# Attention and soft mixture of experts on one core: the turned scores are fetched in whole blocks, exponentials, z, v and weights come at other times

## The chip, the cores and the metric

The kernel runs on one core of a Trainium2 chip. The metric is the device time of one execution in microseconds: the median of three runs of the kernel before is 1449.97 us (1448.82 to 1451.36). The engines are TensorE (PE; PEld is its loading of weights), VectorE (DVE), ScalarE (ACT), GpSimd (POOL) and SyncE (SP). SP computes nothing: every DMA of this kernel is issued by SP, in program order, and SP waits in front of a DMA whose conditions aren't met. ACT and DVE, too, work through their instructions in the order in which the program issues them.

## The reference, cut to what matters

```python
scores = (1 / S) * np.matmul(z, z.transpose(0, 2, 1))     # 8 batches, S = 2496 tokens, z has 64 columns
attn = np.maximum(scores, 0.0) ** 2
x = (u * np.matmul(attn, v)).reshape(N, D)                # N = 19968 tokens, D = 256
logits = x @ phi                                          # 8 experts x 4 slots = 32 columns
d = np.exp(logits - logits.max(0)); d /= d.sum(0) + 1e-09
slot_input = d.T @ x                                      # 32 x 256, 4 slots to each expert
slot_out[e] = np.maximum(slot_input[e] @ w1[e], 0.0) @ w2[e]
c = np.exp(logits - logits.max(1)); c /= c.sum(1) + 1e-09
out = c @ slot_out
```

The score matrix of a batch is symmetric, because keys and queries are the same z. The kernel computes most blocks of it once and turns them over for the other side of the diagonal.

## The kernel before, in words

**Tiling.** A batch has five blocks of up to 512 tokens, and five chunks of queries by the same cut (the last block holds 448 tokens and is padded to 512). A chunk meets the five key blocks one after the other, and each key block in two halves of 256 keys. So a batch is 50 halves, numbered through by `h`; the last batch has 60, because its last chunk of queries is cut in two of 256. The list `MEETS` gives the order of key blocks for each chunk. In every batch but the first, a pair of a chunk and a key block is scored only for the side that comes first. When the other side comes, the half is a turned half: its scores are fetched.

**One half.** `scores` (line 253) gives two PSUM banks of scores, each float32 input split into a high and a low part (three products). In `prepare` (line 288), ACT applies relu with the scale, and squares; then the tile `r` is split again: a cast to `ph` by ACT or DVE, and a subtraction by DVE that gives `pl`. For a pair whose turned side comes later, DVE also turns `r` in squares of 32 x 32 into a tile `y` (line 323 and after), and after both halves of the pair `store` (line 332) writes `y` to a scratch tensor `turned` in HBM, with four DMAs of 256 KB. For a turned half, `fetch` (line 234) has brought `r` from `turned`, and `prepare` only casts and subtracts. `sums_halves` (line 352) or `sums_whole` (line 387, where the half to be prepared is turned) then multiply `ph` and `pl` with the high and low parts of v and add up in `acc`.

**The order of the work** is written out by hand in the loop over `halves` (line 695). While PE sums half `h`, half `h + 3` is prepared. `transfers(h)` (line 641) issues the DMAs: u for the chunk, the fetch for half `h + 5` if that is turned, loads of the next batch's z and v by the tables `z_at` and `v_at` (lines 633 and 634, in halves of the batch), and the stores that have become due. After it, one step of the list `work` runs, if the half is not one of the first two of its chunk. These steps are the mixture's work on a group of 1024 finished tokens (`groups`, line 447): logits on PE and their maxima on DVE; the exponentials on ACT (`exps`); turning x and the exponentials on DVE; four times four DMAs of 72 KB that shift the turned tokens over partitions (`xt<-y`); and the softmax over slots. What a step puts in the list `middle` runs inside the next `prepare`, between relu and square; what it puts in `behind` runs at its end.

**Buffers.** `r` has four, `ph` and `pl` five each, `y` two. z and v of a batch lie in a ring of 16 (`blk`). In the last 20 halves `weights` (line 600) loads the experts' weights, one or two for a half, into buffers that z, v and y leave; 20 of the 32 tiles come before the attention ends, the rest after it.

All compute and DMA instructions but a few pass one helper at line 59, so the rows of the profile name line 59 and are told apart by their tiles: `acc<-ph,v` are the sums, `sc<-z,z` the scores, `r<-turned` a fetch, `turned<-y` a store, `xt<-y` a shift, `zr<-in_zz` and `vr<-in_v` loads of z and v.

Of the kernel before, what the change touches and what calls it, by code (L numbers as in the profile page):

```python
# [34 lines left out]
NWX = 12  # L35
# [27 lines left out]
def attn_soft_moe_kernel(ctx, tc, uT, v, zz, phi, ww, outT):  # L63
# [26 lines left out]
    def take_blocks(b):  # L90


        order = BLOCKS[b == B - 1]
        for j in order[:-1]:
            zt[b, j] = blk.tile([P, 2, 512], F32R, tag="blk", name=f"z_{b}_{j}")
        for i in range(2 * NP):
            vt_[b, i] = blk.tile([P, 2, 2, D], F32R, tag="blk", name=f"v_{b}_{i}")
        j = order[-1]
        zt[b, j] = blk.tile([P, 2, 512], F32R, tag="blk", name=f"z_{b}_{j}")
# [77 lines left out]
    turns_sb = moe.enter_context(tc.tile_pool(name="turns_sb", bufs=2))  # L177
# [68 lines left out]

    def compact(t, x):
        n = x.ch[2]
        if x.padded:
            return t.rearrange("p h (g w) -> p h g w", g=2)[..., 0:PAD]  # L250
        return t[:, :, :n]
# [36 lines left out]
    def prepare(k):  # L288
# [5 lines left out]
        if x.turned:  # L294
            r = arriving.pop(k)
            run(middle)
        else:
            r = wa.tile([P, 2, QC], F32, tag="r", name=f"r_{k}", bufs=4)
            ps, m = scores(k)
            for h in parts:  # L300
                act.activation(r[:, h, :m], ps[:, h, :m], AF.Relu, scale=1.0 / S)
            run(middle)
            for h in parts:
                act.activation(r[:, h, :m], r[:, h, :m], AF.Square)
        hi, lo = (
            wa.tile([P, 2, QC], F32R, tag=t, name=f"{t}_{k}", bufs=5) for t in ("ph", "pl")
        )
        whole = compact(r, x)
        hc, lc = (
            t[:, :, :n].rearrange("p h (g w) -> p h g w", g=2) if x.padded else t[:, :, :n]  # L310
            for t in (hi, lo)
        )
# [35 lines left out]


    side = [0]  # L350

    def sums_halves(k, acc, phase, before):
# [3 lines left out]
        n = x.ch[2]  # L356
# [12 lines left out]
        for i in range(len(todo[0])):  # L369
            for h, rows in enumerate(HALF):  # L370
# [3 lines left out]
                    acc[:, c, :n], vp[rows, c * P : (c + 1) * P], pp[rows, :n],  # L374
# [12 lines left out]
    def sums_whole(k, acc):  # L387

        x = halves[k]
        n = x.ch[2]  # L390
        hi, lo = pend[k]
        for t, kt in enumerate(x.tiles):
            assert kt < KT - 1
            vt = vt_[x.b, kt // 2][:, kt % 2]
            for c in range(2):
                for i, (l, r) in enumerate(((0, hi), (1, hi), (0, lo))):
                    pe.matmul(
                        acc[:, c, :n], vt[:, l, c * P : (c + 1) * P], r[:, t, :n],
# [48 lines left out]
    def groups(q):  # L447
# [17 lines left out]
        def logits():  # L465
# [22 lines left out]
            middle.append(exps)  # L488
# [72 lines left out]
        c1 = lambda: middle.append(combine_exp)  # L561
        rest = lambda: None
        if q < NQG - 2:

            todo = [logits, *blocks, e, shifts[0], c0, shifts[1], c1, shifts[2], c2, shifts[3]]
            todo.append(lambda: (c3(), late.append(slot_sums)))
        else:
# [3 lines left out]
            todo = [*blocks[:2], rest, *blocks[2:], rest, logits, rest, e, lambda: (shifts[0](), add()), *shifts[1:]]  # L571
# [28 lines left out]
    def weights(i):  # L600
# [3 lines left out]
        if i == 0:  # L604
            for _ in range(NBLK):
                take_w(blk, "blk")
            for _ in range(2):
# [3 lines left out]
        order = [[k] for k in (0, 1, 2, 3, 4, 16, 17, 18, 19)] + [[], [], [14, 15]]  # L611
        order += [[k] for k in (13, 11, 12, 5, 6, 7, 8, 9, 10)]
# [26 lines left out]
    landing = {}  # L639

    def transfers(h):
# [4 lines left out]
        if h + 5 < len(halves) and halves[h + 5].turned:  # L646
            fetch(h + 5)
# [47 lines left out]
    for h, x in enumerate(halves):  # L695
# [4 lines left out]
        if last <= 20:  # L700
            weights(20 - last)
# [30 lines left out]
    weights(20)  # L732
    for i in range(NBLK + 4, NW):
# [291 lines left out]
```

## Time and profile before

| | |
|---|---|
| median of three runs | 1449.97 us |
| the profiled execution | 1452.45 us, span 1450.7 us |
| busy PE, DVE, ACT | 1379.0, 1074.7, 909.5 us |
| granted clock of PE over the span | 0.972 |
| DMA packets under 2 KB, of all | 176768 of 255746 |
| HBM read and written | 148.41 and 100.14 MB |

In the page, a group's row ends with the engine's idle time just before its instructions and with what ended that idle time. A row of the timeline has start, length, engine, line, operation, tiles and count; in brackets stands the idle time before it and its releaser. `SPq` is SP as an issuer of DMAs: its rows show how long the issuing took, and the time from issue to landing is listed apart. Each batch takes about 165 to 177 us of the span.

### The profile page before, as it was taken

The numbers are of one execution on the slowest core, as the hardware profiler recorded it, in microseconds if no ns is written. First come the engines' busy times: TensorE is split into PE (matmuls) and PEld (weight loads), VectorE is DVE, ScalarE is ACT, GpSimd is POOL, SyncE is SP. The second block draws the span as 40 slices with busy tenths as digits, with TensorE's granted clock in tenths as the row PEclk, the third lists the DMA queues.
The fourth block names the chain that finished last, engine by engine and source line by source line (L and its number), as shares of the span: only waits on it lengthen the run. The fifth ranks groups of instructions, "written<-read, shape, count | busy, mean of one in ns | idle before, by whom it ended". The sixth has DMA issues, their size and how long they took to land.

```text
span 1450.7 us, 27838 instructions
## 1 busy us (share of the span) xinstructions
PE 1379.0 (95%) x11029; PEld 1090.1 (75%) x11029; DVE 1074.7 (74%) x1401; ACT 909.5 (63%) x1046; POOL 3.7 (0%) x22
## 2 busy tenths in 40 slices
PE   9899999999999999899999999899999999999785
PEld 6677877778777877678777887577877797778653
DVE  6868787858888788577988778585977868686453
ACT  7866686737766576455867477473876566564253
POOL 0000000000000000000000000000000000000000
PEclk9999999999999999899999999999999999999895
DMA  3337567394777845567676945749476866658989
GB/s 125 81 97 188 168 161 228 90 261 139 173 197 214 229 114 163 149 190 209 157 207 155 284 118 127 218 128 268 117 185 183 236 183 167 189 143 249 293 353 389
DMA packets 255746, 272.80 MB, mean 188 GB/s; under 512 B 18560, under 2 KB 176768, under 8 KB 253568
## 3 DMA queue, kind: packets, MB, share of 16 engines
q1 hardware_dynamic: 255616, 271.03, 66.2%
q8 instruction: 86, 1.41, 0.4%
q14 instruction: 44, 0.36, 0.1%
HBM read 148.41 MB, written 100.14 MB: 171 GB/s over the span
## 4 chain that ended last, share of the span: by engine, by line
PE 57%; DVE 12%; DMA 11%; ACT 10%; SPq 6%; issue 4%; DVEq 0%; ACTq 0%
PE acc L59 43%; PE sc L59 9%; DMA r<-turned 7%; SPq L59 6%; ACT r L59 5%; DVE y L59 4%; DVE pl L59 3%; ACT ph L59 3%; DVE z L59 2%; PE pf L59 1%; DMA w<-in_w 1%; PE lg L59 1%; DVE L L59 1%; ACT ot L59 1%; DVE xg L59 1%
## 5 line engine op out<-in xcount | busy, mean ns | idle before, releaser
L59 PE MATMUL acc<-ph,v 64*128 64x512 f32 (+5 forms) x5092 | 996.8, 388 | 16.7 <-ACT ph L59 13.7
L59 PEld LDWEIGHTS acc<-ph,v 64*128 64x128 f32 (+1 forms) x5092 | 608.6, 187 | 162.7 <-issue 19.2
L59 DVE TENSOR_TENSOR pl<-r,ph 128x1024 fp32r<-128x1024 f32 (+2 forms) x412 | 477.8, 1163 | 271.1 <-ACT ph L59 258.1
L59 PE MATMUL acc<-pl,v 64*128 64x512 f32 (+5 forms) x2546 | 630.2, 385 | 3.8 <-DVE pl L59 3.7
L59 ACT CAST ph<-r 128x1024 fp32r<-128x1024 f32 (+2 forms) x259 | 257.1, 997 | 250.5 <-DMA r<-turned 213.2
L59 ACT ACTIVATE r<-sc 128x1024 f32<-128x1024 f32 (+1 forms) x252 | 254.8, 1012 | 174.1 <-PE sc L59 165.1
L59 PEld LDWEIGHTS acc<-pl,v 64*128 64x128 f32 (+1 forms) x2546 | 313.1, 187 | 64.4 <-DVE pl L59 7.2
L59 ACT ACTIVATE r<-r 128x1024 f32<-128x1024 f32 (+1 forms) x252 | 263.6, 1047 | 7.2
L59 DVE STREAM_TRANSPOSE y<-r 128x1024 f32<-128x1024 f32 x152 | 188.0, 1237 | 0.0
L59 PE MATMUL sc<-z,z 64*128 64x512 f32 x960 | 141.9, 397 | 13.3 <-DVE z L59 10.4
L59 DVE CAST ph<-r 128x1024 fp32r<-128x1024 f32 (+2 forms) x153 | 100.3, 656 | 44.9 <-ACT r L59 43.4
L59 PEld LDWEIGHTS sc<-z,z 64*128 64x128 f32 x960 | 89.9, 184 | 40.5 <-DVE z L59 13.9
L59 PE MATMUL sc<-z 64*128 64x512 f32 (+1 forms) x480 | 69.4, 393 | 7.7 <-ACT r L59 7.5
L59 PEld LDWEIGHTS sc<-z 64*128 64x128 f32 x480 | 44.6, 184 | 18.8 <-ACT r L59 11.5
L59 DVE TENSOR_TENSOR v<-vr,v 128x512 fp32r<-128x512 f32 x80 | 54.2, 677 | 3.8 <-ACT v L59 3.7
L59 DVE TENSOR_TENSOR xg<-acc,ut 128x1024 f32<-128x1024 f32 (+7 forms) x57 | 48.6, 876 | 6.0 <-PE acc L59 6.0
L59 DVE STREAM_TRANSPOSE y<-xg 128x512 f32<-128x512 f32 x76 | 52.5, 691 | 0.3 <-DMA xt<-y 0.3
L59 ACT CAST v<-vr 128x512 fp32r<-128x512 f32 x80 | 48.9, 611 | 3.9 <-DMA vr<-in_v 3.7
L59 DVE TENSOR_TENSOR z<-zr,z 64x512 fp32r<-64x512 f32 x70 | 48.1, 687 | 2.1
L59 ACT CAST z<-zr 64x512 fp32r<-64x512 f32 x70 | 43.3, 619 | 5.3 <-DMA zr<-in_zz 3.6
L59 ACT ACTIVATE E<-L,m 128x256 f32<-128x256 f32 x19 | 9.7, 510 | 50.5 <-DVE m L59 50.5
L59 DVE COPY ot<-pf 128x1024 f32<-128x1024 f32 (+2 forms) x22 | 24.3, 1103 | 21.5 <-PE pf L59 20.5
(128 smaller groups left out, 428.3 us busy)
## 6 DMA issues: line engine op xcount, KB each, us to landing
turned<-y SPq DMA_DIRECT2D x304, 256.0 KB, 4.2
r<-turned SPq DMA_DIRECT2D x288, 256.0 KB, 5.0
xt<-y SPq DMA_DIRECT2D x304, 72.0 KB, 3.1
vr<-in_v SPq DMA_DIRECT2D x80, 256.0 KB, 4.4
w<-in_w SPq DMA_DIRECT2D x32, 512.0 KB, 7.4
outT<-ot SPq DMA_DIRECT2D x16, 1024.0 KB, 6.7
ut<-in_uT SPq DMA_DIRECT2D x31, 512.0 KB, 3.8
zr<-in_zz SPq DMA_DIRECT2D x35, 256.0 KB, 4.8
```

Of the source, the lines that this page charges most:

```text
L59: return lambda *a, **k: self.tc.keep_in_program_order(f(*a, **k))
```

## The change

1. `fetch` brings both halves of a turned block with one DMA, whose rows are 8 KB long (4 KB where the queries are only 256), where it was four DMAs with runs of 512 B. The block lies in a buffer of the tag `y`, of which there are three now instead of two; the small ones of the last chunk stay in the four buffers of `r`. `transfers` issues a fetch up to five halves (seven for a small one) before the block's first half. The casts read a half out of the block in runs of 128 elements; in the padded chunk `ph` and `pl` hold 512 columns a half, and the sums read the 448 that count. `ph` and `pl` have four buffers instead of five.
2. `exps` is a step of its own in `work`: it is put in `middle` one step after the logits.
3. In the ring `blk` the last z block stands before v. It is loaded and split at half 33 of the batch before, where it was half 3 of its own batch; the first v tile moves from half 33 to 47, two others by one half.
4. Weights are loaded from the last 30 halves on, five of them before the last 20; 22 come before the attention ends, and `wx` has 10 buffers instead of 12.

```diff
@@ take_blocks
-        order = BLOCKS[b == B - 1]
-        for j in order[:-1]:
+        for j in BLOCKS[b == B - 1]:
             zt[b, j] = blk.tile([P, 2, 512], F32R, tag="blk", name=f"z_{b}_{j}")
         for i in range(2 * NP):
             vt_[b, i] = blk.tile([P, 2, 2, D], F32R, tag="blk", name=f"v_{b}_{i}")
-        j = order[-1]
-        zt[b, j] = blk.tile([P, 2, 512], F32R, tag="blk", name=f"z_{b}_{j}")
@@
-    turns_sb = moe.enter_context(tc.tile_pool(name="turns_sb", bufs=2))
+    turns_sb = moe.enter_context(tc.tile_pool(name="turns_sb", bufs=3))
@@ fetch
-        r = arriving[k] = wa.tile([P, 2, QC], F32, tag="r", name=f"r_{k}", bufs=4)
-        na = 4 * (QC if x.padded else n) // QC
-        for h in range(2):
-            i = 2 * x.w + h
-            sp.dma_start(
-                r[:, h, 0 : na * P].rearrange("p (a r) -> p a r", a=na),
-                scratch[x.b, x.p, j][:, 4 * o // QC : 4 * o // QC + na, i * P : (i + 1) * P],
-            )
+        if n < PAD + PAD:
+            r = wa.tile([P, 2, 4, P], F32, tag="r", name=f"r_{k}", bufs=4)
+        else:
+            r = turns_sb.tile([P, 4, 4, P], F32, tag="y", name=f"r_{k}")
+        a0, na = o // P, r.shape[1]
+        sp.dma_start(
+            r.rearrange("p a j r -> p a (j r)"), scratch[x.b, x.p, j][:, a0 : a0 + na]
+        )
+        for i in range(2):
+            w = halves[k + i].w
+            arriving[k + i] = r[:, :, 2 * w : 2 * w + 2].rearrange("p a h r -> p h a r")
@@ prepare
-            wa.tile([P, 2, QC], F32R, tag=t, name=f"{t}_{k}", bufs=5) for t in ("ph", "pl")
+            wa.tile([P, 2, QC], F32R, tag=t, name=f"{t}_{k}", bufs=4) for t in ("ph", "pl")
...
+        m = QC if x.padded else n
+        hc, lc = (t[:, :, :m].rearrange("p h (a r) -> p h a r", r=P) for t in (hi, lo))
@@ logits in groups
-            middle.append(exps)
@@ groups
-            todo = [logits, *blocks, e, shifts[0], c0, shifts[1], c1, shifts[2], c2, shifts[3]]
+            todo = [logits, ex, *blocks, e, shifts[0], c0, shifts[1], c1, shifts[2], c2, shifts[3]]
@@ weights
-        order = [[k] for k in (0, 1, 2, 3, 4, 16, 17, 18, 19)] + [[], [], [14, 15]]
-        order += [[k] for k in (13, 11, 12, 5, 6, 7, 8, 9, 10)]
+        order = [[], [0], [], [1], [], [2], [], [3], [], [4]]
+        order += [[], [16], [17], [], [18], [19], [], [20], [21], []]
+        order += [[], [15], [14], [12], [13], [6], [7, 5], [8], [9], [10], [11]]
@@
-        z_at = [16, 18 if b > 1 else 40, 21, 31, 53]
-        v_at = [33, 42, 43, 44, 45, 46, 47, 48, 49, 51]
+        z_at = [16, 18 if b > 1 else 40, 21, 31, 33]
+        v_at = [47, 42, 43, 44, 45, 46, 48, 49, 50, 51]
@@ transfers
-        if h + 5 < len(halves) and halves[h + 5].turned:
-            fetch(h + 5)
+        for k in range(h + 1, min(h + 9, len(halves))):
+            y = halves[k]
+
+            if y.turned and y.at % 2 == 0 and k not in arriving and k not in fetched:
+                ahead = 7 if y.ch[2] < PAD + PAD else 5
+                if k - h <= ahead and (y.b, y.p, y.ch[0]) in scratch:
+                    fetched.add(k)
+                    fetch(k)
```

How the change moves instructions shows at three places. The first is SP in chunk 1 of batch 4, from the store of the pair (1, 4) on. `turned_1_2` is the pair of chunk 1 and block 2; `DMAHW` names the lane whose last DMA must have landed, `DVE` and `Activation` the engine whose work must be done. Before:

```order
L59 DMA turned_1_4_8408<-y_8305 32x4x512 [waits DMAHW5_49]
L59 DMA r_8493<-turned_0_1_7962 128x4x128 [waits DMAHW6_49,Activation_49]
L59 DMA r_8493<-turned_0_1_7962 128x4x128 [waits DMAHW7_49]
L59 DMA r_8539<-turned_0_1_7962 128x4x128 [waits DMAHW0_49,DVE_49,Activation_49]
L59 DMA r_8539<-turned_0_1_7962 128x4x128 [waits DMAHW1_49]
L59 DMA zr_0_8557<-in_zz 128x512 [waits DMAHW2_49]
L59 DMA turned_1_2_8559<-y_8392 32x4x512 [waits DMAHW3_49,DVE_49]
L59 DMA turned_1_2_8559<-y_8392 32x4x512 [waits DMAHW4_49]
L59 DMA turned_1_2_8559<-y_8392 32x4x512 [waits DMAHW5_49]
L59 DMA turned_1_2_8559<-y_8392 32x4x512 [waits DMAHW6_49]
L59 DMA r_8605<-turned_0_2_8057 128x4x128 [waits DMAHW7_49,DVE_49,Activation_49]
L59 DMA r_8605<-turned_0_2_8057 128x4x128 [waits DMAHW0_49]
```

And with the change:

```order
L59 DMA turned_1_4_8264<-y_8161 32x4x512 [waits DMAHW1_49]
L59 DMA r_8346<-turned_0_1_7819 128x2048 [waits DMAHW4_49,DMAHW3_49,DMAHW2_49]
L59 DMA zr_0_8407<-in_zz 128x512 [waits Activation_49]
L59 DMA turned_1_2_8409<-y_8248 32x4x512 [waits DVE_49]
L59 DMA turned_1_2_8409<-y_8248 32x4x512 [waits DMAHW5_49]
L59 DMA turned_1_2_8409<-y_8248 32x4x512 [waits DMAHW6_49]
L59 DMA turned_1_2_8409<-y_8248 32x4x512 [waits DMAHW7_49]
L59 DMA r_8456<-turned_0_2_7912 128x2048 [waits DMAHW6_49,DMAHW5_49,DMAHW7_49,DMAHW4_49,DMAHW0_49]
L59 DMA zr_1_8475<-in_zz 128x512 [waits DMAHW1_49,Activation_49]
L59 DMA turned_1_3_8477<-y_8378 32x4x512 [waits DMAHW2_49,DVE_49]
L59 DMA turned_1_3_8477<-y_8378 32x4x512 [waits DMAHW3_49]
```

The four DMAs of a block have become one, and the second block waits for the four stores in front of it (lanes 4 to 7), whose `y` gives it its buffer.

The second is the same place in batch 5, with the change only, where shifts stand between:

```order
L59 DMA r_10189<-turned_0_1_9671 128x2048 [waits DMAHW4_49]
L59 DMA xt<-y_9836 32x576 [waits DMAHW5_49]
L59 DMA zr_0_10251<-in_zz 128x512 [waits DMAHW1_49,Activation_49]
L59 DMA turned_1_2_10253<-y_10131 32x4x512 [waits DMAHW2_49,DVE_49]
L59 DMA turned_1_2_10253<-y_10131 32x4x512 [waits DMAHW5_49]
L59 DMA r_10299<-turned_0_2_9803 128x2048 [waits DMAHW6_49,DVE_49]
L59 DMA xt<-y_9836 32x576 [waits DMAHW7_49]
L59 DMA zr_1_10321<-in_zz 128x512 [waits DMAHW3_49]
L59 DMA turned_1_3_10323<-y_10222 32x4x512 [waits DMAHW4_49]
L59 DMA turned_1_3_10323<-y_10222 32x4x512 [waits DMAHW7_49]
L59 DMA r_10352<-turned_1_2_10253 128x2048 [waits DMAHW0_49]
```

Of each four stores only the first and the last are shown, and of four shifts the first. Here the second block takes the buffer of the first one and waits for DVE, its last reader; the third stands behind shifts, a z load and stores.

The third is ACT in chunk 1 of batch 4, around the exponentials `E`. Before:

```order
L59 ACTIVATE r_8464<-sc_8465 128x1024
L59 ACTIVATE E_8473,m_8320<-L_8446,m_8320 128x256
L59 ACTIVATE m_8320<-m_8320 128x1
L59 ACTIVATE r_8464<-r_8464 128x1024
L59 CAST ph_8477<-r_8464 128x1024
L59 ACTIVATE r_8509<-sc_8510 128x1024
```

With the change:

```order
L59 ACTIVATE r_8320<-sc_8321 128x1024
L59 ACTIVATE r_8320<-r_8320 128x1024
L59 CAST ph_8330<-r_8320 128x1024
L59 ACTIVATE r_8361<-sc_8362 128x1024
L59 ACTIVATE E_8370,m_8176<-L_8302,m_8176 128x256
L59 ACTIVATE m_8176<-m_8176 128x1
L59 ACTIVATE r_8361<-r_8361 128x1024
```

The exponentials stand one half later, again between relu and square.

More of the change, by code (lines that the diff above doesn't have):

```diff
@@ L34 @@
 CATCH = 12
-NWX = 12
+NWX = 10
 BLOCKS = (0, 1, 2, 3, 4), (4, 0, 1, 2, 3)
@@ L294, in prepare @@
         if x.turned:
-            r = arriving.pop(k)
+            whole = arriving.pop(k)
             run(middle)
@@ L304, in prepare @@
                 act.activation(r[:, h, :m], r[:, h, :m], AF.Square)
+            whole = r[:, :, :m].rearrange("p h (a r) -> p h a r", r=P)
         hi, lo = (
-            wa.tile([P, 2, QC], F32R, tag=t, name=f"{t}_{k}", bufs=5) for t in ("ph", "pl")
+            wa.tile([P, 2, QC], F32R, tag=t, name=f"{t}_{k}", bufs=4) for t in ("ph", "pl")
         )
[L308 to L312, printed above, removed]
+        m = QC if x.padded else n
+        hc, lc = (t[:, :, :m].rearrange("p h (a r) -> p h a r", r=P) for t in (hi, lo))
         cast = act.copy if x.turned or (x.turns and x.at % 3) else dve.tensor_copy
@@ L347, in await_, with columns, totals @@
         )
+    def columns(t, x):
+        if x.padded:
+            return t.rearrange("p (g w) -> p g w", g=2)[:, :, 0:PAD]
+        return t[:, : x.ch[2]]
+    def totals(acc, c, x):
+        n = x.ch[2]
+        return acc[:, c, :n].rearrange("p (g w) -> p g w", g=2) if x.padded else acc[:, c, :n]
     side = [0]
@@ L355, in sums_halves @@
         x = halves[k]
-        n = x.ch[2]
         todo = [[], []]
@@ L373, in sums_halves @@
                 mm = pe.matmul(
-                    acc[:, c, :n], vp[rows, c * P : (c + 1) * P], pp[rows, :n],
+                    totals(acc, c, x), vp[rows, c * P : (c + 1) * P], columns(pp[rows], x),
                     start=(x.begins and phase == 0 and i == 0),
@@ L389, in sums_whole @@
         x = halves[k]
-        n = x.ch[2]
         hi, lo = pend[k]
@@ L397, in sums_whole @@
                     pe.matmul(
-                        acc[:, c, :n], vt[:, l, c * P : (c + 1) * P], r[:, t, :n],
+                        totals(acc, c, x), vt[:, l, c * P : (c + 1) * P], columns(r[:, t], x),
                         start=(x.begins and t == 0 and i == 0),
@@ L560, in groups @@
         e, c0, c2, c3 = (lambda f=f: behind.append(f) for f in (turn_e, combine, combine_sum, combine_turn))
-        c1 = lambda: middle.append(combine_exp)
+        ex, c1 = (lambda f=f: middle.append(f) for f in (exps, combine_exp))
         rest = lambda: None
         if q < NQG - 2:
-            todo = [logits, *blocks, e, shifts[0], c0, shifts[1], c1, shifts[2], c2, shifts[3]]
+            todo = [logits, ex, *blocks, e, shifts[0], c0, shifts[1], c1, shifts[2], c2, shifts[3]]
             todo.append(lambda: (c3(), late.append(slot_sums)))
@@ L570, in groups @@
             add = lambda: behind.append(adding.pop(0))
-            todo = [*blocks[:2], rest, *blocks[2:], rest, logits, rest, e, lambda: (shifts[0](), add()), *shifts[1:]]
+            todo = [*blocks[:2], rest, *blocks[2:], rest, logits, ex, e, lambda: (shifts[0](), add()), *shifts[1:]]
             todo += [c0, c1, c2, c3]
@@ L606, in weights @@
                 take_w(blk, "blk")
-            for _ in range(2):
+        if i == 10:
+            for _ in range(3):
                 t = turns_sb.tile([P, 16, 4, NS], F32, tag="y", name=f"w_{len(w_raw)}")
@@ L638, in attn_soft_moe_kernel @@
             splits.setdefault(base + at, []).append((load_v, b, i))
-    landing = {}
+    landing, fetched = {}, set()
     def transfers(h):
@@ L699, in attn_soft_moe_kernel @@
         transfers(h)
-        if last <= 20:
-            weights(20 - last)
+        if last <= 30:
+            weights(30 - last)
         for f in landing.pop(h, ()):
@@ L731, in attn_soft_moe_kernel @@
     wx = exx.enter_context(tc.tile_pool(name="wx", bufs=NWX, side="right", reuse_waits="tile"))
-    weights(20)
-    for i in range(NBLK + 4, NW):
+    weights(30)
+    for i in range(NBLK + 6, NW):
         take_w(wx, "wx")
```

5 lines of the change are left out of this document (removed).

## The prediction

> **What bounds the kernel now.** I read the busy times first, then the waits, then stretches of the span, one per batch, and last single instructions of the stretches that are too long.
>
> ```profile
> PE 1379.0 (95%) x11029; PEld 1090.1 (75%) x11029; DVE 1074.7 (74%) x1401; ACT 909.5 (63%) x1046; POOL 3.7 (0%) x22
> ```
>
> TensorE (PE) is busy for 95% of 1450.7 us, so all that can be won without taking work from it is its 71.7 us of idle time and what its clock loses. The next table has one row per batch, cut at the same place in each: the first score matmuls of chunk 0 against key block 4, which is the place where PE waits for a split of z. Columns: length, then busy time of PE, PEld, DVE, ACT and POOL, then the granted clock, DMA share, GB/s.
>
> ```profile
> 203.77:369.07 165.30, 161.30 (x1238) 129.16 (x1239) 126.73 (x159) 108.56 (x121) 0.00 (x0) 0.99 0.67 180
> 369.07:535.01 165.94, 162.00 (x1302) 131.12 (x1302) 130.43 (x174) 109.32 (x124) 0.00 (x0) 1.00 0.71 189
> 535.01:711.73 176.72, 167.93 (x1240) 133.06 (x1240) 130.58 (x167) 108.82 (x122) 0.00 (x0) 0.96 0.62 169
> 711.73:876.42 164.69, 161.72 (x1302) 131.20 (x1302) 130.31 (x174) 109.08 (x124) 0.00 (x0) 1.00 0.72 191
> 876.42:1051.40 174.98, 166.15 (x1239) 130.97 (x1240) 130.83 (x167) 109.03 (x122) 0.00 (x0) 0.96 0.64 172
> 1051.40:1216.02 164.62, 160.57 (x1302) 130.50 (x1302) 129.67 (x174) 108.55 (x124) 0.00 (x0) 1.00 0.73 194
> 1342.00:1376.00 34.00, 25.52 (x210) 21.78 (x208) 13.85 (x31) 8.36 (x15) 0.79 (x2) 0.85 0.90 288
> ```
>
> Batches 4 and 6 take 164.7 us, batches 3 and 5 take 176.72 and 174.98. The excess is 12.0 + 10.3 = 22.3 us, at a clock of 0.96. The last row, the end of the attention, has PE idle for 8.5 of 34 us at a clock of 0.85. Who is waited for:
>
> ```profile
> ACT ph L59 <- DMA r<-turned: 213.2, 103, 7.1
> ACT E L59 <- DVE m L59: 50.5, 19, 7.1
> PE acc L59 <- ACT ph L59: 13.7, 7, 3.8
> PE sc L59 <- ACT r L59: 10.5, 14, 1.8
> PE sc L59 <- DVE z L59: 10.4, 8, 2.5
> ```
>
> ScalarE's 213.2 us for the fetched turned scores are not a gain in themselves: only 13.7 us come out at PE as a wait for ph. Here is one such stall in batch 1, and two in batch 3 with what the DMA queue did around them and the granted clock after the first:
>
> ```profile
> 308.63 0.73 PE L59 MATMUL acc<-ph,v 128*128 128x512 f32 x2 [1.87 <-ACT ph L59]
> 584.93 0.74 PE L59 MATMUL acc<-ph,v 128*128 128x512 f32 x2 [2.21 <-ACT ph L59]
> 610.36 1.32 PE L59 MATMUL sc<-z 64*128 64x512 f32 x6 [1.84 <-ACT r L59]
> 571.55 3.81 SPq L59 DMA_DIRECT2D turned<-y  x4
> 575.41 3.50 SPq L59 DMA_DIRECT2D xt<-y  x4
> 579.02 2.60 SPq L59 DMA_DIRECT2D r<-turned  x4
> 581.66 0.62 SPq L59 DMA_DIRECT2D zr<-in_zz  x1
> 582.32 3.49 SPq L59 DMA_DIRECT2D turned<-y  x4
> 585.85 3.68 SPq L59 DMA_DIRECT2D xt<-y  x4
> 589.63 2.60 SPq L59 DMA_DIRECT2D r<-turned  x4
> 588.00:592.00 4.00, 4.00 (x22) 2.74 (x22) 2.60 (x3) 1.43 (x3) 0.00 (x0) 0.71 0.55 157
> ```
>
> SP issues without a gap: from one fetch of two halves to the next it needs 3.81 + 3.50 + 2.60 + 0.62, about 10.6 us. PE needs two turned halves in 5.6 us (priced below). So in this stretch the issuing of DMAs on one queue is the bound, and each PE stall costs clock after it (0.71 in the 4 us after the 2.21 us gap). In batches 4 and 6 the shifts (xt) fall elsewhere, and the same stretch holds.
>
> [...]
>
> **The change, part by part.** *The fetch.* A block was four DMAs of 256 KB in rows of 512 B; it is one DMA of 1 MB in rows of 8 KB. The nearest rows are the stores of the result (1 MB, also 8 KB rows):
>
> ```profile
> turned<-y SPq DMA_DIRECT2D x304, 256.0 KB, 4.2
> L59 SPq DMA_DIRECT2D r<-turned x320: 359/621/2435, 76.2 to 1366.1; - x160
> DMA to landing us min/median/max: 2.4/4.9/8.5
> L59 SPq DMA_DIRECT2D outT<-ot x22: 332/332/461, 1397.2 to 1443.3; - x22
> DMA to landing us min/median/max: 3.2/6.6/8.3
> ```
>
> SP's time for a block falls from about 2.6 us to about 0.4, and the cycle of batch 3 from 10.6 to 8.3 us per block. That alone would still be over 5.6 us; but only two such cycles follow each other, and the first fetch starts early, so the backlog is about 2 × 2.7 us against a lead of five halves. The 320 fetches become 80.
>
> *The new wait.* Blocks now share a ring of three with the tiles in which VectorE (DVE) turns scores (y). In even batches the second block of chunk 1 takes the slot of y(1,2): SP waits until four stores have landed. In odd ones it takes that of the first block, and waits for its last reader. In batch 4 (the row without an engine's tile is from the chain of waits):
>
> ```profile
> 745.03 2.79 SPq L59 DMA_DIRECT2D turned<-y  x4
> 748.91 4.05 SPq L59 DMA_DIRECT2D r<-turned  x4
> 715.03 0.70 PE sc L59 x6
> 745.86 0.73 PE L59 MATMUL acc<-ph,v 128*128 128x512 f32 x2
> 759.97 0.63 PE L59 MATMUL acc<-ph,v 128*128 128x512 f32 x2
> ```
>
> Five halves of 2.8 us lie between 745.86 and 759.97, and the half that starts at 759.97 is the first to use this block. The fourth store is issued near 747.1 and lands after 4.2 at 751.3. The fetch follows at 751.4 and takes L, then 1.05 us for the cast and 1.22 for the subtraction: ready at 753.7 + L against 759.97. L is not in the trace. Lower bound: the 370 GB/s that the tail moves make 2.8 us of 1 MB, plus 1.7 (the fastest r fetch, 2.4, less 0.7 for its 256 KB at that rate), 4.5 us. Upper bound: 8.3, the slowest outT. I take 5.5, nearer the lower end, since SP has waited for the stores and little else is in flight. Ready at 759.2: no stall; at 8.3 a stall of 2.0 us. In odd batches the block's slot is free 2.3 us after the half two before it, so it is ready 2.5 + 5.5 + 2.3 = 10.3 us after that point, against 11.2; but the third block there stands behind four shifts, a z load and four stores (3.5 + 0.6 + 3.6 us), is ready at 18.4 and needed at 17.5 (five halves of 2.8 and one of 3.5, with its six score matmuls of 0.70). With the clock, about 2 us in each of batches 3 and 5. Behind SP's wait stand stores, z loads and shifts; the next stores free y slots for DVE, with a lead of three halves. In the long runs of 14 turned halves the slot is free five halves before the data is needed, 14 us against 5.5 + 2.3.
>
> [...]
>
> So the fetch gives 22.3, and 1.9 for the stall in batch 1, less 4: **20.2 us**.
>
> *Exponentials half a step later.* ScalarE stood behind DVE's chain of maxima between relu and square, and PE's next scores behind the square:
>
> ```profile
> 267.59 0.97 PE L59 MATMUL sc<-z 64*128 64x512 f32 x6 [0.93 <-ACT r L59]
> 1210.74 0.97 PE L59 MATMUL sc<-z 64*128 64x512 f32 x6 [1.36 <-ACT r L59]
> ```
>
> Of the 10.5 us of such PE waits 1.84 are counted in batch 3; the others come from this chain (0.93 and 1.36 here, more at two places) or from late fetches. All 50.5 us of ScalarE's wait lie beside PE except these. The list of MoE steps grows from 14 to 15; 1024 tokens are 20.5 halves, in 8 of 10 of which a step may run, 16.4, so nothing piles up. I take **5 us** of the 8.7.
>
> *z earlier.* The split of the last z block moves from DVE's densest chunk to a stretch of turned halves. PE's waits for z are 10.4 us, seven of the eight at the edges of the table above and one in batch 0, which does not change. DVE stays the busiest beside PE there, and its subtractions are late next: **7 us**. v follows up to one half later, which keeps at least one half of 2.8 us before its use against 0.61 + 0.68 us for a split.
>
> *The end of the attention.*
>
> ```profile
> 1353.85 0.50 PE L59 MATMUL acc<-ph,v 128*128 128x256 f32 x2 [2.72 <-ACT ph L59]
> 1367.70 0.50 PE L59 MATMUL acc<-ph,v 128*128 128x256 f32 x2 [3.77 <-ACT ph L59]
> ```
>
> Here small fetches stood behind weights. They now come as one DMA for two, up to seven halves ahead, and five weights are loaded before. The last fetch needs a slot that comes free late, and the weights of the last halves press together, so I take **5 us** of 6.5 and the clock.
>
> *At nothing.* Casts and subtractions of the padded chunk work on 1024 instead of 896 elements:
>
> ```profile
> L59 ACT CAST ph<-r 128x1024 fp32r<-128x1024 f32 x184 | 191.8, 1049 | 151.7 <-DMA r<-turned 129.4 <-PE acc L59 12.6 <-DVE pl L59 2.9
> L59 ACT CAST ph<-r 128x896 fp32r<-128x896 f32 x59 | 55.4, 940 | 62.9 <-DMA r<-turned 52.9 <-PE acc L59 4.3 <-DVE pl L59 3.5
> ```
>
> That is 0.11 us on 59 casts, 6.4 us of ScalarE beside 62.9 us of idleness; without cover it would cost those 6.4. The 896 were read in two strided runs at 1.05 ns per element against 1.02, so the new runs of 128 elements cost little. Four ph/pl buffers instead of five let the casts run three halves ahead, 8.4 us for 2.3 us of work.
>
> **Sum.** 20.2 + 5 + 7 + 5 = 37.2 us. The profiled execution took 1452.45 us (span 1450.7 and 1.75 around it); the median of the runs is 1449.97, 2.5 lower. 1452.45 − 37.2 is 1415.2; less the 2.5, the median should be **1413 us**.
>
> **Rivals.** *SP stays the bound.* Stores and shifts, 7.3 of the 10.6 us, remain, so batches 3 and 5 might keep most of their excess. Then the fetch gives 8 instead of 20.2: 1425 us. For it speaks the gapless SP; against it, that batches 4 and 6 hold with the same fetches.
>
> *Blocks land late.* At L = 8.3 batches 1, 2, 4 and 6 stall by 2.0 at the second block, batches 3 and 5 by 3.7 over the second and third, with about 2 us of slower clock after each stall: 4 × 4 + 2 × 7.7 = 31, less the 4 counted, 27 us more: 1440 us. For it the tail, where 1 MB takes 6.6 at the median; against it, that there several are in flight.
>
> *Slower: the ring locks SP and DVE together.* SP waits for a slot, the stores behind it wait, y slots come free late, DVE stands in front of its turn with the subtractions behind it, and the next block is later still. From a landing of about 10 us on, the even batches lose 3.7 us at the second block and each delay reaches the next store. If then all six batches take 176.7 as batch 3 did, they last 1060 against 1012.3 us: 48 more, less 17 from the other parts: 1481 us. Against it: no fetch so far took over 8.5 us.
>
> *No clock to win back.* If the slow clock is no consequence of the gaps, batches 3 and 5 give only their idle time over that of batch 4 (PE idle 8.8 in each, against 3.0), 11.6 of 22.3: 1424 us. The 0.71 after the gap speaks against it. [...]
>
> **Chances.** Forecast 60%, own range 1401 to 1423; SP stays the bound 16; late blocks 11; locked ring 8; no clock 3; nothing gained on balance 2. A run of this kernel can be told from no change at about 0.2% (the three runs span 2.5 us). Faster: all of the first, second and fifth and most of the third, 88%; same 4%; slower 8%. The range that leaves out two in ten reaches from 1401 over the late blocks to 1440.
>
> **What would show it.** Batches 3 and 5 at or below 165 us with a clock of 1.00; 80 fetches with a landing of 5 to 6 us; ScalarE's wait for r far under 213.2; no wait of PE for z from batch 1 on; E's wait under 5 us; PE busy 97% or more. I am wrong if SP waits long for landed stores ahead of r, if DVE y waits for DMA, or if waits of PE for ph are 10 us or more.

## The result, and the profile after

The changed kernel takes 1409.57 us (median of four runs, 1407.84 to 1410.43) against 1449.39 us for the kernel before beside it: a ratio of 0.9724, with an interval of 0.9707 to 0.9742, or 39.8 us. The profiled execution took 1410.43 us with a span of 1408.7 us, 42.0 us below the one before.

The busy times of the page:

```profile
PE 1362.1 (97%) x11029; PEld 1079.7 (77%) x11029; DVE 1085.8 (77%) x1401; ACT 913.8 (65%) x1046; POOL 4.2 (0%) x22
```

The same batches as in the prediction, cut at the same score matmuls (columns as there: length, busy PE, PEld, DVE, ACT, POOL, granted clock, DMA share, GB/s):

```profile
201.77:362.70 160.93, 160.05 (x1240) 128.36 (x1238) 127.65 (x159) 108.84 (x122) 0.00 (x0) 1.00 0.63 186
362.70:523.67 160.97, 160.97 (x1305) 129.42 (x1302) 132.72 (x174) 110.17 (x125) 0.00 (x0) 1.00 0.64 192
523.67:691.09 167.42, 162.65 (x1242) 130.15 (x1239) 131.24 (x166) 108.93 (x123) 0.00 (x0) 0.98 0.63 181
691.09:852.05 160.96, 160.96 (x1304) 129.39 (x1302) 132.70 (x174) 110.18 (x125) 0.00 (x0) 1.00 0.65 192
852.05:1019.80 167.75, 162.31 (x1240) 130.40 (x1238) 131.23 (x166) 108.87 (x123) 0.00 (x0) 0.98 0.63 181
1019.80:1179.49 159.69, 159.66 (x1305) 129.47 (x1302) 132.40 (x174) 110.72 (x125) 0.00 (x0) 1.00 0.67 197
1179.49:1408.70 229.21, 200.51 (x1867) 152.55 (x1863) 142.61 (x201) 111.11 (x141) 1.23 (x2) 0.89 0.78 269
```

Against the rows of before the six batches are shorter by 4.4, 5.0, 9.3, 3.7, 7.2 and 4.9 us, 34.5 in all; what lies ahead of them by 2.0, and what follows by 5.5. So the gain is spread. In the four batches that the prediction took to be in order, 165 us became 161 or less; batches 3 and 5, from which it expected 20 us, gained 16.5, and still stand 6.5 and 6.8 us above batch 4. PE is without a gap in batches 2 and 4 (busy for 160.97 of 160.97 and 160.96 of 160.96 us).

The waits of the changed kernel:

```profile
ACT ph L59 <- DMA r<-turned: 130.0, 42, 9.1
ACT ph L59 <- PE acc L59: 63.6, 47, 4.0
ACT E L59 <- DVE m L59: 16.7, 7, 2.8
PE lg L59 <- DVE xg L59: 10.3, 4, 4.6
PE sl L59 <- DMA xt<-y: 5.7, 1, 5.7
PE sc L59 <- DVE z L59: 1.4, 1, 1.4
PE sc L59 <- ACT r L59: 1.3, 3, 0.7
PE acc L59 <- ACT ph L59: 0.8, 1, 0.8
```

PE's three waits of before (13.7 us for ph, 10.5 for r, 10.4 for z) are down to 3.5 us together. Two others lead now in the attention: for xg (a chunk's finished tokens, `acc` times `u`) ahead of the logits, and for a shift ahead of the last slot sums. The first is where batches 3 and 5 lose. It is not new; in the kernel before, PE waited for xg in the same two batches, 2.05 us in batch 3 (at 596.61) and 4.62 us in batch 5 (at 937.79):

```profile
PE lg L59 <- DVE xg L59: 6.7, 2, 4.6
```

Here are PE's gaps in those batches and at the end of the changed kernel, by the timeline:

```profile
570.95 0.74 PE L59 MATMUL acc<-ph,v 128*128 128x512 f32 x2 [0.76 <-ACT ph L59]
582.55 1.51 PE L59 MATMUL lg<-xg,phi_sb 64*32 64x256 f32 x20 [3.49 <-DVE xg L59]
911.37 1.52 PE L59 MATMUL lg<-xg,phi_sb 64*32 64x256 f32 x22 [4.57 <-DVE xg L59]
1322.85 2.31 PE L59 MATMUL sl<-xt 64*32 64x256 f32 x32 [5.67 <-DMA xt<-y]
```

With a gap of 0.52 us for pl behind the first row, and one before the third, the gaps in chunk 1 are 4.8 us in batch 3 and 5.1 us in batch 5. The same waits (ph, pl and xg) were 4.8 and 5.7 us in the kernel before. So the stretch that the prediction set out to cure has hardly changed.

SP around the second and third block of chunk 1 in batch 3:

```profile
550.75 0.66 SPq L59 DMA_DIRECT2D r<-turned  x1
...
556.02 4.75 SPq L59 DMA_DIRECT2D turned<-y  x4
563.52 0.34 SPq L59 DMA_DIRECT2D r<-turned  x1
563.90 2.68 SPq L59 DMA_DIRECT2D xt<-y  x4
567.25 3.71 SPq L59 DMA_DIRECT2D turned<-y  x4
571.01 0.47 SPq L59 DMA_DIRECT2D r<-turned  x1
```

And DVE and ACT there, at the first block's last reading and when the third block has come:

```profile
561.13 2.36 DVE L59 TENSOR_TENSOR pl<-r,ph 128x1024 fp32r<-128x1024 f32 x2 [0.72 <-ACT ph L59]
...
579.73 1.99 ACT L59 CAST ph<-r 128x1024 fp32r<-128x1024 f32 x2 [6.60 <-DMA r<-turned]
580.80 1.23 DVE L59 TENSOR_TENSOR pl<-r,ph 128x1024 fp32r<-128x1024 f32 x1 [5.73 <-ACT ph L59]
581.95 1.28 DVE L59 TENSOR_TENSOR xg<-acc,ut 128x384 f32<-128x384 f32 x2
```

The stores end at 560.8, but the second block is issued only at 563.52: its slot is the first block's, which DVE reads until 563.49. Behind it stand a shift, a load and four stores, so the third block is issued at 571.01 and cast 8.7 us later. DVE's multiplication that ends the chunk (xg) stands in program order behind the subtraction for that block, and PE's logits behind the multiplication. So the late block comes out at PE mostly as a wait for xg, not for ph.

### The profile page after: what moved, and what is told of

It is laid out like the page before. It is cut to its first block, busy times and chain, and to the rows that moved or that the text cites. A ratio compares the mean times of both kernels' runs of the same rounds, so it can differ in the third digit from the quotient of the medians.

```text
span 1408.7 us, 27263 instructions
## 1 busy us (share of the span) xinstructions
PE 1362.1 (97%) x11029; PEld 1079.7 (77%) x11029; DVE 1085.8 (77%) x1401; ACT 913.8 (65%) x1046; POOL 4.2 (0%) x22
## 3 DMA queue, kind: packets, MB, share of 16 engines
q1 hardware_dynamic: 106368, 271.02, 63.6%
## 4 chain that ended last, share of the span: by engine, by line
PE 83%; DMA 7%; ACT 3%; DVE 3%; issue 2%; SPq 1%; ACTq 0%; DVEq 0%
PE acc L59 65%; PE sc L59 11%; DMA r<-turned 5%; PE lg L59 3%; PE pf L59 2%; SPq L59 1%; DMA xt<-y 1%; ACT r L59 1%; ACT ot L59 1%; DVE pl L59 1%; ACT ph L59 1%; DVE y L59 1%; PE po L59 1%; PE h L59 1%; DVE xg L59 0%
## 5 line engine op out<-in xcount | busy, mean ns | idle before, releaser
L59 PEld LDWEIGHTS acc<-ph,v 64*128 64x128 f32 (+1 forms) x5092 | 600.6, 186 | 150.7 <-issue 19.7
L59 DVE TENSOR_TENSOR pl<-r,ph 128x1024 fp32r<-128x1024 f32 (+1 forms) x412 | 488.3, 1191 | 196.4 <-ACT ph L59 180.8
L59 ACT CAST ph<-r 128x1024 fp32r<-128x1024 f32 (+1 forms) x259 | 260.7, 1021 | 204.8 <-DMA r<-turned 130.0
L59 PEld LDWEIGHTS acc<-pl,v 64*128 64x128 f32 (+1 forms) x2546 | 308.4, 185 | 62.5 <-DVE pl L59 4.2
L59 DVE CAST ph<-r 128x1024 fp32r<-128x1024 f32 (+1 forms) x153 | 102.1, 667 | 57.3 <-ACT r L59 56.6
L59 PE MATMUL sc<-z,z 64*128 64x512 f32 x960 | 138.9, 393 | 2.3 <-DVE z L59 1.4
L59 DVE COPY ot<-pf 128x1024 f32<-128x1024 f32 (+2 forms) x22 | 24.3, 1104 | 21.7 <-PE pf L59 21.7
L59 ACT COPY ot<-pf 128x1024 f32<-128x1024 f32 (+2 forms) x22 | 20.1, 915 | 25.6 <-PE pf L59 25.6
```

The source lines that it names most:

```text
L59: return lambda *a, **k: self.tc.keep_in_program_order(f(*a, **k))
```

## The experiments

Each kernel was timed beside the kernel before. Ratios are to that; a ratio of 0.0100 is 14.5 us, and the changed kernel stands at 0.9724. Gains or losses against it are differences of ratios, with both intervals taken together.

### Which part is worth what

**The exponentials with the logits again.**

```diff
             dve.tensor_scalar_mul(m[:, 1:2], mnew, -1.0)
+            middle.append(exps)
...
-            todo = [logits, ex, *blocks, e, shifts[0], c0, shifts[1], c1, shifts[2], c2, shifts[3]]
+            todo = [logits, *blocks, e, shifts[0], c0, shifts[1], c1, shifts[2], c2, shifts[3]]
...
```

> The exponentials go back into the step of the logits; everything else is as changed. The prediction's shares (exponentials 5 us): 1414.6 us, with E waiting for m as long as before (about 50 us) and about 7 us of PE waits for r in stretches with scores. Rival, from cutting both traces at the same places (batches 1, 2, 4 and 6 became 3.6 to 5.0 us shorter although they hardly had a wait for a fetch): the exponentials and z together are worth 24 us, so this kernel takes about 1421 us and every batch is about 2 us longer than with the change. Third possibility, nothing: 1409.6, if the waits for r came from late fetches only.

1425.07 us, 0.9842 (0.9812 to 0.9872): 17 ± 5 us slower than the change, three times the prediction's size and more than the rival's 12. Two of its waits:

```profile
ACT E L59 <- DVE m L59: 52.9, 18, 5.4
PE sc L59 <- ACT r L59: 10.5, 13, 2.4
```

Both are back where they were before (50.5 and 10.5), although the fetches are the new ones. So nearly all of PE's waits for r came from the place of the exponentials, and hardly any from late fetches.

**The same, with an empty step in their place**, so that the turning and the shifts stay where the change has them:

```diff
+            middle.append(exps)
...
-            todo = [logits, ex, *blocks, e, ...
+            todo = [logits, rest, *blocks, e, ...
```

> The exponentials go back into the step of the logits, but an empty step stands in their place, so that all later steps of a group (the turning, the shifts) stay where the change has them. If the place of the exponentials on ScalarE is what counts (PE's next scores wait for r, which waits behind E): about 1425 us, as with the exponentials back and no empty step, batches 2, 4 and 6 near 164 us. If the half step by which all later steps move is what counts: 1409.6 us, batches 2, 4 and 6 at 161 us. A split between the two is possible.

1420.08 us, 0.9813 (0.9790 to 0.9835): 13 ± 4 us slower than the change. PE's waits for r are 8.1 us. So most of the 17 us is the place on ScalarE. The other 4 us would be what it is worth that all later steps of a group come one half later; they are within both intervals.

**That later place alone, in the kernel before** (one empty step, so the shifts of a group come one half later):

```diff
-            todo = [logits, *blocks, e, shifts[0], ...
+            todo = [logits, rest, *blocks, e, shifts[0], ...
```

> The kernel before with an empty step behind the logits and nothing else: exponentials, z, fetches and weights as before, but the shifts of a group come one half later. In chunk 1 of batches 3 and 5 the second and third shift then stand behind the fetch of their half and no longer in the half before, ahead of it. If that order on SP made the excess of these batches: 176.7 and 175.0 us become 169 to 171, the others stay at 165: 1437 to 1440 us. If the excess came from the exponentials themselves, from z or from the form of the fetch: 1449 us.

1444.3 us, 0.9982 (0.9970 to 0.9995): 2.6 us faster, not 10. SP does do what was expected (timeline, chunk 1 of batch 3):

```profile
562.86 1.97 SPq L59 DMA_DIRECT2D r<-turned  x2
564.88 2.59 SPq L59 DMA_DIRECT2D xt<-y  x4
...
573.04 2.18 SPq L59 DMA_DIRECT2D r<-turned  x2
```

The shifts stand behind the first half of a fetch now. But the cycle from fetch to fetch is still 10.2 us, and PE waits 4.08 and 4.43 us for xg in those places. In the profiled execution batches 3 and 5 take 171.6 and 174.0 us (176.7 and 175.0 before). So this order of SP's queue takes away a part of their excess over batch 4 and leaves the larger part, 15.7 of 22.3 us.

**z and v back** for batches 1 to 6 (the last z block at half 53, behind v in the ring):

```diff
-        z_at = [16, 18 if b > 1 else 40, 21, 31, 33]
-        v_at = [47, 42, 43, 44, 45, 46, 48, 49, 50, 51]
+        z_at = [16, 18 if b > 1 else 40, 21, 31, 53]
+        v_at = [33, 42, 43, 44, 45, 46, 47, 48, 49, 51]
...
```

> For the batches 1 to 6 the last z block and the first v tiles are loaded and split where they were before; batch 7 stays as changed. The prediction's shares (z 7 us): about 1416 us, with a PE wait for z in each of six batches. Rival (z and the exponentials together 24 us, because each gap costs clock as well): about 1421 us, each batch 2 us longer.

1417.67 us, 0.9781 (0.9759 to 0.9803): 8 ± 4 us slower, with PE waiting 8.4 us for z instead of 1.4. The prediction had 7.

**The weights from the last 20 halves on, as before:**

```diff
-        if last <= 30:
-            weights(30 - last)
+        if last <= 20:
+            weights(20 - last)
...
```

> The weights are loaded from the last 20 halves on, one for a half, as before; their buffers stay those of the change. Prediction (5 us for the end, weights and small fetches together): up to 1414.6 us, if all of the gain is due to the weights, and 1409.6 if it is due to the small fetches that come as one DMA and earlier. Rival: the stretch from batch 6 on became 6.5 us shorter, and the shifts near the end already stand behind weights, so with more weights in that place the wait of the slot sums grows: 1416 us or more.

1410.92 us, 0.9736 (0.9716 to 0.9756): 1.7 ± 3.9 us, not to be told from nothing. The new places of the weights bring little.

**Exponentials and z in the kernel before, and nothing else.** The edits are the change's own in `groups` and in `z_at`, `v_at` and `take_blocks`, the latter for batches 1 to 6:

```diff
-            middle.append(exps)
...
-            todo = [logits, *blocks, e, shifts[0], ...
+            todo = [logits, ex, *blocks, e, shifts[0], ...
...
-        z_at = [16, 18 if b > 1 else 40, 21, 31, 53]
+        z_at = [16, 18 if b > 1 else 40, 21, 31, 33]
...
```

> The kernel before with two parts of the change only: the exponentials a half step later, and z and v in their new places for batches 1 to 6. Fetches, buffers and weights are as before. The prediction's shares (5 + 7): 1438 us. Rival (24 us for the two, 18 for fetch and end): 1426 us, batches 1, 2, 4 and 6 at 161 us, batches 3 and 5 at 171 to 173 us.

1421.44 us, 0.9811 (0.9793 to 0.9829): 27.4 us of the 40 without any new fetch. Its stretches, cut at the same places (batches 2, 3 and 5, and what follows batch 6):

```profile
364.25:525.10 160.85, 160.85 (x1306) 131.48 (x1303) 131.01 (x174) 109.57 (x125) 0.00 (x0) 1.00 0.72 192
525.10:694.24 169.14, 163.05 (x1240) 129.77 (x1238) 130.12 (x166) 108.76 (x123) 0.00 (x0) 0.98 0.67 180
...
855.09:1024.16 169.07, 162.81 (x1240) 129.85 (x1238) 130.21 (x166) 108.90 (x123) 0.00 (x0) 0.98 0.67 180
1183.26:1419.40 236.14, 203.17 (x1867) 153.38 (x1863) 143.22 (x202) 112.18 (x142) 1.23 (x2) 0.89 0.78 261
```

With the old fetches batches 2 and 4 are at 160.85 us already. Beside it the rest of the change wins 1.7 and 1.3 us in batches 3 and 5 (169.14 to 167.42, 169.07 to 167.75), 3.4 us over all six batches, and 6.9 us in what follows (236.14 to 229.21).

**Exponentials and z both back in the changed kernel**, by the two edits above together, so the fetch and the weights alone:

> Exponentials and z both back where they were, so the fetch and the weights alone. If the parts add up: 1408.7 + 17 + 8 = 1434 us on the scale of these runs, and 1436 by what the two gave alone (27 us). If fetch and exponentials take the same stalls away twice over (each alone would cure batches 3 and 5), the two back cost more than their sum: 1440 us or more. The prediction's shares (12 us for the two): 1421 us.

1438.68 us, 0.9920 (0.9888 to 0.9951): 28 ± 5 us slower than the change, and 11.6 us faster than before. 17 + 8 is 25, the two alone gave 27.4: over the whole kernel the parts add up within what can be measured. In batches 3 and 5 they overlap, by the profiled executions: the fetch and the weights alone bring these two to 171.52 and 172.47 us, a gain of 7.7 us together, and exponentials and z alone gained 13.5 us there, but all of them together only 16.5.

### What the fetch does

**One block in four DMAs again**, with everything else as changed:

```diff
-        sp.dma_start(
-            r.rearrange("p a j r -> p a (j r)"), scratch[x.b, x.p, j][:, a0 : a0 + na]
-        )
+        for i in range(4):
+            sp.dma_start(r[:, :, i], scratch[x.b, x.p, j][:, a0 : a0 + na, i * P : (i + 1) * P])
```

> The changed kernel, but each block is fetched by four DMAs with runs of 512 B again; ring, lead and everything else as changed. SP needs about 2.6 us for a block again instead of 0.4. The prediction's theory (SP's issuing in chunk 1 is the bound of batches 3 and 5, and the shorter fetch gave some 20 us): about 1425 us or more, batches 3 and 5 at 175 us. New theory, from the kernel before with exponentials and z alone, whose batches take 160.9 us with the old fetches and 169.1 for 3 and 5: the form of the fetch is worth 2 us in each of batches 3 and 5 and up to 7 at the end: 1412 to 1420 us, batches 2, 4 and 6 unchanged at 161 us.

1424.47 us, 0.9823 (0.9802 to 0.9844): 14 ± 4 us slower. That is the time that the prediction's theory named, but not its place. From here on stretches run from the first run of whole sums in chunk 1 of a batch to that of the next batch, or from the last chunks to the end. Batch 3 and the last chunks, with four DMAs:

```profile
559.81:726.73 166.92, 162.72 (x1304) 129.50 (x1303) 132.28 (x174) 109.98 (x126) 0.00 (x0) 1.00 0.70 190
1215.96:1421.80 205.84, 166.75 (x1567) 124.79 (x1565) 112.52 (x168) 84.04 (x114) 1.22 (x2) 0.86 0.82 273
```

And with one:

```profile
555.92:725.41 169.49, 164.72 (x1304) 131.22 (x1302) 132.23 (x174) 109.48 (x126) 0.00 (x0) 0.98 0.65 187
1216.25:1408.70 192.45, 163.75 (x1567) 122.55 (x1565) 112.39 (x168) 83.85 (x114) 1.23 (x2) 0.87 0.82 291
```

Both kernels reach the last chunks at 1216 us: over the batches the form of the fetch is worth nothing. In batch 3 the four DMAs are even 2.6 us better. Their third block starts 16.2 us into the stretch (576.01), and its first half is cast at 581.47, 21.7 us into it; with one DMA it starts at 15.1 and is cast at 23.8, since both halves land together (8.6 us after the issue, and cast one behind the other). All of the loss, 13.4 us, is at the end. There SP issues (timeline, four DMAs):

```profile
1286.87 3.18 SPq L59 DMA_DIRECT2D r<-turned  x4
1290.60 2.42 SPq L59 DMA_DIRECT2D xt<-y  x4
```

while the small block of the change takes 0.5 us (1309.60 to 1310.13, for one). The longest PE waits there are 8.0 us for the slot sums' shift, 4.9 for xg and 4.1 for pl; with one DMA they are 5.7, 1.8 and under 0.4. So in this kernel the one DMA pays at the end, where SP has shifts, weights and many blocks at once. How much of the 13.4 us is SP's time and how much the transfer in runs of 512 B was not tested apart.

### What holds batches 3 and 5 back

**Two moves.** In groups 6 and 11 the third and fourth shift come after the third fetch of chunk 1; in the last group but one the logits come one step earlier:

```diff
+            if q in (6, 11):
+                todo[-4:] = [c1, c2, c3, shifts[2]]
+                todo.append(lambda: (shifts[3](), late.append(slot_sums)))
+            else:
+                todo.append(lambda: (c3(), late.append(slot_sums)))
...
-            todo = [*blocks[:2], rest, *blocks[2:], rest, logits, ex, e, ...
+            todo = [*blocks[:2], rest, *blocks[2:], logits, ex, e, ...
```

> The changed kernel with two moves. In groups 6 and 11 (batches 3 and 5) the third and fourth shift come after the third fetch of chunk 1 instead of before it and after it; in the last group but one the logits come one step earlier, and with them everything up to the slot sums. Theory (the third block stands behind shifts, z and stores on SP, and DVE's multiplication of x stands behind its subtraction): PE's waits for xg in batches 3 and 5 go, and with them the slow clock after them, so both take 161 to 163 us instead of 167.5: 10 to 13 us; PE's wait for the slot sums' shifts (5.7 us) goes: 5 to 7 us. Together 1389 to 1394 us. Rival (the block's landing of 8 us and the slot that it waits for decide): the stalls in batches 3 and 5 stay, 1402 us. Second rival for the end (the shifts stand behind weights on SP, and come no earlier): the wait of 5.7 us stays.

1399.74 us, 0.9658 (0.9632 to 0.9683): 9.6 ± 4.5 us faster than the change, though less than the 15 us or more that were expected. The stretches of batches 3 and 5:

```profile
555.08:720.32 165.24, 162.20 (x1304) 129.28 (x1303) 132.05 (x174) 109.47 (x126) 0.00 (x0) 1.00 0.66 192
879.21:1044.51 165.30, 162.34 (x1305) 129.34 (x1303) 132.14 (x174) 109.49 (x126) 0.00 (x0) 1.00 0.66 192
```

They were 169.49 and 169.82. PE's waits for xg fall to 1.62 and 1.55 us, and the clock is back at 1.00; the wait for the slot sums' shift falls from 5.67 to 2.13. The third block starts 11.2 us into the stretch instead of 15.1.

**A ring of four** (r with two buffers pays for it, and small blocks partly lie in one buffer of the ring), with the moves:

```diff
-NWX = 10
+NWX = 9
...
-    turns_sb = moe.enter_context(tc.tile_pool(name="turns_sb", bufs=3))
+    turns_sb = moe.enter_context(tc.tile_pool(name="turns_sb", bufs=4))
...
-            r = wa.tile([P, 2, 4, P], F32, tag="r", name=f"r_{k}", bufs=4)
+            if small[0] % 4 < 2:
+                r = wa.tile([P, 2, 4, P], F32, tag="r", name=f"r_{k}", bufs=2)
+            else:
+                if small[0] % 4 == 2:
+                    two[:] = [turns_sb.tile([P, 2, 2, 4, P], F32, tag="y", name=f"r_{k}")]
+                r = two[0][:, small[0] % 2]
+            small[0] += 1
...
```

> The kernel with the two moves, and a ring of four buffers for blocks and turned scores instead of three (r has two buffers instead of four, of the small blocks every second pair lies in one buffer of the ring, and wx has nine buffers). The second block of chunk 1 in batches 3 and 5 then needs no longer wait for the last reader of the first. If the wait for the slot is what is left there: PE's waits of 0.9 + 0.5 for the second block and 1.6 us for xg go in both batches, with the clock about 4 us each: 1391 to 1393 us. If the landing of the blocks (9 to 10 us there, beside eight shifts) decides: little is won, 1397 to 1400 us. The end may lose 1 to 3 us, since the small blocks come later.

1398.69 us, 0.9668 (0.9650 to 0.9686). The stretch of batch 3 falls to 162.7 us, so without the wait for the slot it is 2.6 us shorter; the last chunks lose as much as is won. Freeing the halves of that buffer singly:

```diff
-                if small[0] % 4 == 2:
+                if small[0] == 2:
```

> The kernel with the two moves and a ring of four; unlike the ring of four before, the two halves of the one buffer for small blocks are taken and freed singly. If the 5 us that the last chunk lost there (114.1 us from its first run of whole sums of batch 7 on became about 121) came from small blocks that wait for a pair: 1392 to 1395 us, with the PE waits for pl (1.9) and for the slot sums (4.1) down to 0.4 and 2.1. If they come from r with two buffers: 1398 us as before.

1397.84 us, 0.9652 (0.9639 to 0.9665); batch 3 at 162.98, batch 5 at 163.48. The wait for the slot sums' shift stays at 4.1 us, so pairs were not the cause at the end. The versions with the moves cannot be told from each other; all are 8 to 10 us below the change.

**The ring of four without the moves**, that is the last kernel's edits of `fetch` and the pools on the changed kernel:

```diff
-            todo = [*blocks[:2], rest, *blocks[2:], logits, ex, e, ...
+            todo = [*blocks[:2], rest, *blocks[2:], rest, logits, ex, e, ...
```

and the order of groups 6 and 11 as in all the others.

> The changed kernel with the ring of four and without the two moves, so the third and fourth shift stay where the change has them. If the wait for the slot made the stalls in chunk 1 of batches 3 and 5: both fall from 169.5 and 169.8 (from one chunk 1 to the next) to 163, as with moves and ring: 1396 to 1398 us. If the shifts ahead of the third block are as much at fault: 165 to 167 in each, 1400 to 1405 us.

1408.83 us, 0.9722 (0.9707 to 0.9738): the time of the change. Batches 3 and 5 take 166.98 and 166.80 us (169.49 and 169.82 with three buffers), but the last chunks take 196.51 us instead of 192.45, with a PE wait of 8.4 us for the slot sums' shift. SP, chunk 1 of batch 3:

```profile
560.12 0.86 SPq L59 DMA_DIRECT2D r<-turned  x1
...
569.86 0.64 SPq L59 DMA_DIRECT2D r<-turned  x1
```

The second block starts 3.4 us earlier by the clock of the trace, the third only 1.2, since shifts and stores fill SP between them. So of the excess that the change leaves in a batch (169.49 and 169.82 against 163.01 in batch 1), the ring alone takes 2.5 and 3.0 us, the shifts' place alone 4.3 and 4.5, and both together 6.5 and 6.3: all of it in batch 3, and nearly all in batch 5.

## Why the prediction was right in sum and wrong in its parts

The forecast of 1413 us was 3.4 us too high, inside its own range. That is luck: two errors of opposite sign and similar size hide in it, 12 to 17 us too much for the fetch and about 12 too little for the exponentials.

**The fetch, 20.2 us, is the step that failed.** It put the whole excess of batches 3 and 5 (22.3 us) down to SP's issuing for fetches. In its place the runs show 3.4 us over all batches for fetch and ring beside exponentials and z, and 7.7 us in batches 3 and 5 without these; with one DMA or four in the new ring, the batches take the same time. What had been read rightly was the queue: gapless, 10.6 us from fetch to fetch. The wrong step led from the shorter issue (0.4 us for a block instead of 2.6; the median of the 80 is 0.52) to a backlog that fits into the lead of five halves. SP's 7 us of shifts, loads and stores between two blocks remained; the new wait for the slot used up what the shorter fetch saved (third block 15.1 us into the stretch, against 15.6 with old fetches); and one landing for both halves made the first half later (cast 23.8 us into the stretch, against 21.7 with four DMAs). That is the rival "SP stays the bound": batches 3 and 5 kept 13.3 of their 22.3 us. Its 1425 us did not come, because another term was larger.

**The stalls of batches 3 and 5** were placed rightly, at the third block behind shifts, a load and stores, with about 2 us each; PE's gaps there are 4.8 and 5.1 us (0.76, 0.52 and 3.49; 0.52 and 4.57). The missed link is DVE: the chunk's multiplication stands behind the late block's subtraction. It could have been read before the change, from PE's 6.7 us of waits for xg, which the prediction doesn't list. The landing failed there too: 8.7 us from issue to cast instead of 5.5.

**The exponentials** were the mis-sized term: 5 us forecast, 17 ± 5 measured, most of it from the place on ScalarE. About 9 of the 10.5 us of PE's waits for r belonged to them (10.5 with the exponentials back, 1.3 with the change). In the profiled executions PE is idle 10.9 us longer with the exponentials back, and busy 4.6 us longer, for which no run shows the cause. The prediction set some of the 10.5 us aside for late fetches and took a part of the rest.

**z** held (7 against 8 ± 4). **The end** held in size (5 against 5.2 from 1216.02 to 1374.16 before and 1179.49 to 1332.46 after, each up to the last sums), and as far as the runs show through the fetches (13.4 us more there with four DMAs) and not through the weights (1.7 ± 3.9). **What was put at nothing** held for the buffers: ScalarE's waits for ph behind PE rose from 19.9 to 63.6 us with four buffers, but PE's waits for ph are 0.8 us in all, so the cover was enough.

**The ring in even batches** held. Batch 4, SP and then ACT:

```profile
723.25 2.89 SPq L59 DMA_DIRECT2D turned<-y  x4
729.37 0.34 SPq L59 DMA_DIRECT2D r<-turned  x1
```

```profile
734.93 2.00 ACT L59 CAST ph<-r 128x1024 fp32r<-128x1024 f32 x2 [4.31 <-DMA r<-turned]
```

The block waits for the stores, starts 4.0 us into the stretch (5.5 forecast) and lands in 5.5 us (5.5 forecast); no stall. That is not the usual landing:

```profile
L59 SPq DMA_DIRECT2D r<-turned x80: 319/524/1986, 76.9 to 1315.4; - x80
DMA to landing us min/median/max: 4.5/7.6/11.1
```

The fastest, 4.5 us, is a small block of 512 KB; those of 1 MB take 4.9 us at least, just above the lower bound of 4.5, and up to 11.1, so the upper bound of 8.3 is passed. Blocks did land late, then, as that rival had it, but it reached PE only in batches 3 and 5, mostly at the third block. The argument "little else is in flight" holds in batch 4, where SP has waited for its stores (5.5 us), and not beside four shifts (third block: 8.6 us in batch 3, 9.4 in batch 5).

**The signs.** Right: the 80 fetches, z, ScalarE's wait for r (130.0 us), PE at 97%, and none of the three named as proof of error in any size (SP waits 3.2 us for stores ahead of the fetch in batch 4, about as reckoned; DVE y waits 2.5 us for a shift, once). Wrong: batches 3 and 5 are at 167 us and a clock of 0.98, the landing is 7.6 us, E's wait is 16.7 us instead of under 5, of which 1.3 us at most reach PE. The rival without clock to win back is answered by the two moves: with shorter gaps in batches 3 and 5 their clock is 1.00 instead of 0.98.

## What to carry to other kernels

A busy queue beside a stall is not yet its price: ask at which time the late transfer would start if the suspected cost were gone, with everything that stays in the queue and with the slot that it needs. Waits that show up small in every batch can be worth more than a large one in two: moving the exponentials and z, behind 10.5 and 10.4 us of waits for r and z in pieces of 0.3 to 2.5 us, gave two thirds of the gain, while PE's gaps in the conspicuous stretch hardly shrank (4.8 and 5.7 us before, 4.8 and 5.1 after). Then follow a late transfer through the engines that work in order: here it came out at PE under another tile's name. And where one total is forecast from several terms, take them back one by one, since two wrong terms can meet in a right sum.

## What the runs showed of the hardware that was not expected

The clock after a gap of PE. Each row covers the 4 us after a gap. In the kernel before, gaps of 1.84 and of 2.54 us:

```profile
610.36:614.36 4.00, 4.00 (x22) 3.17 (x24) 3.96 (x7) 3.12 (x3) 0.00 (x0) 0.57 0.42 91
535.01:539.01 4.00, 4.00 (x22) 3.17 (x24) 3.65 (x5) 3.13 (x3) 0.00 (x0) 0.58 0.11 30
```

In the changed kernel, a gap of 1.84 us:

```profile
1233.25:1237.25 4.00, 4.00 (x82) 2.91 (x84) 3.83 (x6) 0.51 (x1) 0.00 (x0) 1.00 0.70 222
```

And in the kernel with the empty step alone, one of 2.53 us, at the same place of the program as the 2.54 above:

```profile
535.67:539.67 4.00, 4.00 (x34) 3.27 (x36) 3.05 (x4) 3.14 (x3) 0.00 (x0) 1.00 0.24 58
```

So two gaps of the same length gave 0.57 and 1.00, and two others 0.58 and 1.00. In the attention, from 100 us into the span on, the traces of the kernel before and of the changed one have five gaps of 3.49 us or more, and each left a clock of 0.60 or less in the next 4 us (0.50 for the 3.49, 4.57 and 5.67 us of the changed kernel and the 4.62 us before, 0.60 for the 3.77 us before). Of the nine gaps from 1.69 to 2.72 us, eight left 0.57 to 0.76, and the one of 1.84 us in the changed kernel 1.00; those from 0.60 to 1.37 us all left 1.00. The gap of 2.21 us in the prediction belongs to the middle group, with 0.74 right after it; the row of 0.71 that the prediction shows for it starts 3.1 us later.
